# Attention in 64-row groups: scores as split products, transposes as two halves, spread reciprocals, v products in three pieces

## The chip, the cores and the metric

The kernel runs on one core of a Trainium2 chip. The metric is the time of one execution on the device in microseconds (us), the median of several runs. PE is the matrix engine (its weight loads have a row of their own, PEld), DVE the vector engine, ACT the scalar engine, POOL the GpSimd engine, SP the engine whose queue issues most DMAs.

## What is computed

Three stages follow one another. The first is attention with a learned bias, for 4 batches, 8 heads, 576 positions, head size 64; the second and third are dense layers over the 4 x 576 = 2304 tokens of width 512.

```python
scores = scale * np.matmul(q, k.transpose(0, 1, 3, 2))
...
scores = scores + bias.transpose(2, 0, 1)[None, :, :, :]
scores = scores - np.max(scores, axis=-1, keepdims=True)
attn = np.exp(scores)
attn = attn / (np.sum(attn, axis=-1, keepdims=True) + 1e-09)
return np.matmul(attn, v).astype(np.float32)
...
x = np.ascontiguousarray(attn_out.transpose(0, 2, 1, 3)).reshape(B * S, H * D)
x = _moe_ref(x=x, **moe_kwargs)
return _moe2_ref(x=x, **moe2_kwargs)
```

The middle layer multiplies by 512 x 1024 weights, applies h * softmax(h) and a layer norm, and multiplies by 1024 x 512 weights. The last one multiplies by 512 x 2048 weights, applies a clipped square, and multiplies by 2048 x 512 weights. All is float32; large products are made of a high part in the PE format fp32r and a low remainder.

## The kernel before

A head part (up to about 52 us) makes the bias and writes it to DRAM. Then come 16 **units**, one for each head pair `hp` and batch `b` (`u = 4 * hp + b`), then the middle layer (18 blocks of 128 tokens), then the last layer. The change touches attention, and the transposes and outputs of the middle layer.

**Inputs.** `load_qk` (L213) brings q and k of one head, each as [64, 640] and each stored twice, in partitions 0 to 63 and 64 to 127, with one DMA of 640 KB into one of two stage buffers. `prep_all` (L228) is a generator of four steps per head: DVE casts k to `kh`, the remainder goes to `kl` (DVE for the first unit, POOL later), DVE casts q to `sq`, and the lower 64 partitions of `sq` become the remainder of q. So `sq` holds the high part of q in 64 rows and the low part in the other 64, and two products over 128 rows, with `kh` and with `kl`, give the whole score.

**A unit** has nine row blocks `n` of 128 rows: four for each head, and block 8 with the last 64 rows of both. `k = 9 * u + n`.
- `emit_qk` (L379): the matmuls of a block (L392), 288 columns each, into the two banks of `ps_s` (two such buffers): 4, or 8 for block 8. Then one DVE instruction (L398) adds the bias, writes the negated scores `e` and takes their minimum into `su`.
- `emit_exp` (L410): ACT's exponential in place, with the row sums into `su`.
- `emit_T` (L486): four 128x128 transposes of a block into a bank of `ps_t` (three buffers, L497), copied to `pt` by ACT (L498); single blocks for the columns 512 to 575 (L504, L505, L511), copied by ACT and, for block 8, by DVE (L507, L508).
- `emit_pv` (L514): products with v (L529), 64 rows of output for each head, 256 columns at a time in two groups, and 64 columns for block 8. ACT copies the first 512 columns to `xb` (L536), DVE the last 64 (L538).
- `emit_norm` (L460): `r` makes the reciprocals of the row sums on DVE (L464, L465) and spreads them over 64 columns on POOL (L466); `R` transposes them on PE (L474), `M` multiplies `xb` by them on DVE (L476); `S` and `N` do the same for block 8 (L479, L484).

**The order** is written by hand: one string of letters for each of the nine blocks (`order`, L621), in which Q is `emit_qk`, E `emit_exp`, T the transposes of the block five before, P the v products of a group seven before, B a step of `prep_all`, W a step of the splitting of the middle layer's weights (`split_w`, L311), and r, R, M, S, N the normalization of the unit before. Every engine takes its instructions in this order. After the last block the same loop runs on with `tail`, mixed with the first two token blocks of the middle layer (`emit_h`, `emit_post`).

**The middle layer** uses the same PSUM pool: `emit_h` takes a `ps_s`, `emit_lt` (L821) transposes eight 128x128 blocks (L835) into two `ps_t`, and `emit_o` (L844) puts 48 products (L854) into `ps_x`, which has one buffer.

Of the kernel before, what the change touches and what calls it, by code (L numbers as in the profile page):

```python
# [28 lines left out]
QW = S + 64  # L29
NU = HP * B  # L30
# [8 lines left out]
def tile_attention_moe_moe(  # L39
# [168 lines left out]
    EB, LT, LP = 4, 5, 7  # L208


    kh_t, kl_t, sq_t, v_t, stg_t = {}, {}, {}, {}, {}

    def load_qk(s, eng=nc.sync):  # L213
        if s < 2 * NU:
            u, h = divmod(s, 2)
            hp, b = divmod(u, B)
            st = wq.tile([128, 2 * QW], F32, tag="stg", name="stg", bufs=2)
            eng.dma_start(out=st, in_=qk[b, 2 * hp + h])
            stg_t[s] = st
# [7 lines left out]

    def prep_all():  # L228
        for s in range(2 * NU):
            u, h = divmod(s, 2)  # L230
            st = stg_t.pop(s)
            n = S + 64 * h
            kh = wq.tile([128, n], F32R, tag=f"kh{h}", name="kh", bufs=2)
            kl = wq.tile([128, n], F32R, tag=f"kl{h}", name="kl", bufs=2)
            sq = wq.tile([128, QW], F32R, tag="sq", name="sq", bufs=4)
            ks = st[:, QW:QW + n]
            nc.vector.tensor_copy(kh, ks)
            yield
            eng = nc.vector if u == 0 else nc.gpsimd
            eng.tensor_tensor(out=kl, in0=ks, in1=kh.bitcast(F32), op=ALU.subtract)  # L240
            nc.vector.tensor_copy(sq, st[:, 0:QW])  # L241
            yield
            eng.tensor_tensor(
                out=sq[64:128], in0=st[64:128, 0:QW], in1=sq[64:128].bitcast(F32), op=ALU.subtract
            )
            kh_t[s], kl_t[s], sq_t[s] = kh, kl, sq
            load_qk(s + 2)
            yield
            yield

# [126 lines left out]
    e_t, su_t, r_t, pt_t, x_t = {}, {}, {}, {}, {}  # L377

    def emit_qk(k, sc=None):  # L379
        u, n = divmod(k, 9)  # L380
        hp, b = divmod(u, B)
        sc = sc or ps_s()
        i, h0 = divmod(n, 2)
        for hf in range(2):
            parts = []
            for h in ([h0] if n < 8 else [0, 1]):
                lhs = sq_t[2 * u + h][:, 128 * i:128 * i + 128]
                c0 = hf * HS + (64 if h == 1 and n == 8 else 0)
                for kk in (kh_t[2 * u + h], kl_t[2 * u + h]):
                    parts.append((lhs, kk[:, c0:c0 + HS]))  # L390
            for j, (l, r) in enumerate(parts):
                nc.tensor.matmul(sc[:, hf, 0:HS], lhsT=l, rhs=r, start=j == 0, stop=j == len(parts) - 1)  # L392
        if n % 2 == 0:
# [3 lines left out]
        e = e_t[u, i][:, h0, :]  # L397
        nc.vector.tensor_tensor_reduce(  # L398
            out=halves(e),
            in0=sc[:, :, 0:HS],  # L400
# [19 lines left out]
    for p in range(NB + 2):  # L420
# [9 lines left out]
        if p in first:  # L430
            emit_qk(first[p], ps0.tile([128, 2, 512], F32, tag="zz", name="zz", bufs=1))
        elif p - 1 in first:
            emit_exp(first[p - 1])
# [20 lines left out]
    def ps_t():  # L454
        return ps.tile([128, 512], F32, tag="t", name="ps_t", bufs=3)

    def ps_x():
        return ps.tile([128, 512], F32, tag="x", name="ps_x", bufs=1)

    def emit_norm(u, c):  # L460
        su, x = su_t[u], xb_t[u % B][:, u // B] if c in "MN" else None
        rc = su[:, 18:27]
        if c == "r":
            nc.vector.tensor_scalar(out=rc, in0=su[:, 9:18], scalar1=1e-9, scalar2=None, op0=ALU.add)  # L464
# [5 lines left out]
        elif c == "R":  # L470
            r_t[u] = r = ps_t()
            rb = flat(e_t.pop((u, 4)))[:, S:S + 512]
            for i in range(4):
                nc.tensor.transpose(r[:, 128 * i:128 * i + 128], rb[:, 128 * i:128 * i + 128], ident)  # L474
        elif c == "M":
            nc.vector.tensor_tensor(out=x[:, 0:512], in0=x[:, 0:512], in1=r_t.pop(u), op=ALU.mult)  # L476
        elif c == "S":
            r_t[u, 1] = r = ps_t()
            nc.tensor.transpose(r[:, 0:128], rc[:, 8:9].to_broadcast([128, 128]), ident)  # L479
        elif c == "N":  # L480
            r = r_t.pop((u, 1))
            for h in range(2):
                hs = slice(64 * h, 64 * h + 64)
                nc.vector.tensor_tensor(out=x[hs, 512:S], in0=x[hs, 512:S], in1=r[hs, hs], op=ALU.mult)  # L484

    def emit_T(k):  # L486
        u, n = divmod(k, 9)
        i, h = divmod(n, 2)
        e = flat(e_t[u, i])
        g, o = divmod(i, 2)  # L490
        if n in (0, 4, 8):
            pt_t[u, g] = wa.tile([128, 9, 256], F32, tag="pt", name="pt", bufs=2)
        pt = pt_t[u, g]
        tp = ps_t()
        for kt in range(4):
            c0 = (S + 64) * h + kt * 128
            nc.tensor.transpose(tp[:, kt * 128:(kt + 1) * 128], e[:, c0:c0 + 128], ident)  # L497
# [16 lines left out]
    def emit_pv(u, g):  # L514
# [4 lines left out]
        if g != 1:  # L519
            x_t[u] = ps_x() if g == 0 else ps_t()  # L520
# [104 lines left out]
    for k in range(NK + LP + 1):  # L625
# [32 lines left out]
        if k > NK:  # L658
            step(bp)
# [561 lines left out]
```

## Time and profile before

| | |
|---|---|
| median of 3 runs | 916.93 us (915.68 to 918.5) |
| the profiled execution, its own time | 915.25 us |
| its span, first to last instruction | 913.5 us |
| head, up to the first steady matmuls of attention | about 52 us |
| attention with its end | about 52 to 325 us |
| middle layer | about 325 to 532 us |
| last layer | about 532 to 913.5 us |
| PE, DVE, ACT, POOL busy | 902.6, 711.9, 604.1, 255.8 us |

The profile is of one execution. A duration of DVE or ACT runs from its start to the acknowledgement of its last write, so that one instruction overlaps the next a little. The ends of matmuls are modelled and they overlap much, so that the distance from one start to the next tells more than the duration. The chain that ended last is followed back from the last instruction; a piece of it counts the time from its start to the next piece's.

### The profile page before, as it was taken

To read this page: it belongs to the slowest core of one execution; us is meant where nothing else is said; L and a number is where in the kernel's file an instruction comes from. 1 tells how busy PE (TensorE), PEld (TensorE's weight loads), DVE (VectorE), ACT (ScalarE), POOL (GpSimd) and SP (SyncE) were. 2 spreads that over 40 slices of the span, in tenths; PEclk is the share of its full clock that TensorE was granted. 3 is DMA by queue.
4 is the path that set the end of the run, shared out by engine and by line. 5 is a ranking of instruction groups with operands and counts; after the bars stand their busy time and mean duration, and the time that the engine had idled before them with its cause. 6 is when DMAs were issued, how large, how long until landed. Compare 5 with 4: busy or idle time off the path is not lost.

```text
span 913.5 us, 17850 instructions
## 1 busy us (share of the span) xinstructions
PE 902.6 (99%) x6538; PEld 791.3 (87%) x6538; DVE 711.9 (78%) x1534; ACT 604.1 (66%) x1262; POOL 255.8 (28%) x231
## 2 busy tenths in 40 slices
PE   9989999999999999999999999999999999999998
PEld 6668888888888889999999998888898889888896
DVE  9968888989898548888988258888887875677864
ACT  7889898999999766677676544655455443455442
POOL 1036566565755223545366400000000000000000
PEclk9999999999999999999999999999999999999999
DMA  6994654744741102555653678769577765448541
GB/s 192 315 318 128 204 179 152 240 149 140 245 158 51 36 24 94 185 197 185 242 206 137 223 252 308 263 198 326 171 233 252 264 222 162 124 150 257 172 161 70
DMA packets 102523, 173.21 MB, mean 190 GB/s; under 512 B 11618, under 2 KB 66402, under 8 KB 102436
## 3 DMA queue, kind: packets, MB, share of 16 engines
q1 hardware_dynamic: 96000, 165.70, 55.2%
q10 hardware_dynamic: 6068, 4.73, 1.5%
q0 software_dynamic: 368, 1.64, 0.5%
q8 instruction: 52, 0.85, 0.4%
q14 instruction: 35, 0.29, 0.1%
HBM read 125.49 MB, written 46.54 MB: 188 GB/s over the span
## 4 chain that ended last, share of the span: by engine, by line
PE 80%; DVE 7%; ACT 6%; issue 3%; DMA 2%; POOL 1%; ACTq 0%; DVEq 0%; SPq 0%
PE acc L1026 20%; PE ab L988 18%; PE ps_s L392 10%; PE ps_x L529 8%; PE ps_t L497 7%; PE ps_s L575 6%; PE ps_x L854 4%; DMA bias_d<-ow 2%; ACT r L286 1%; POOL wp L723 1%; PE ps_s L854 1%; DVE wp L720 1%; PE ps_t L474 1%; PE ps_t L529 1%; DVE wp L712 1%
## 5 line engine op out<-in xcount | busy, mean ns | idle before, releaser
L1026 PE MATMUL acc<-wo,gh 128*128 128x512 f32 x576 | 179.3, 392 | 0.0
L398 DVE CUSTOM_DVE_ANT_0 e<-ps_s,bt 128x576 f32<-128x576 f32 x143 | 106.9, 748 | 20.2 <-PE ps_s L392 16.3
L1026 PEld LDWEIGHTS acc<-wo,gh 128*128 128x128 f32 x576 | 105.8, 188 | 14.5 <-DVE ob L1011 0.7
L413 ACT ACTIVATE e<-e,su 128x576 f32<-128x576 f32 x144 | 112.6, 782 | 7.4 <-DVE su L398 6.8
L1026 PE MATMUL acc<-wo,gl 128*128 128x512 f32 x288 | 114.5, 398 | 0.3 <-DVE gl L975 0.3
L392 PE MATMUL ps_s<-kh,sq 128*128 128x288 f32 x318 | 100.3, 333 | 3.3 <-ACT ow L303 2.0
L974 ACT CAST gh<-ga 128x384 fp32r<-128x384 f32 x96 | 49.4, 515 | 75.0 <-DVE ga L968 75.0
L498 ACT COPY pt<-ps_t 128x512 f32<-128x512 f32 x144 | 83.6, 582 | 10.5 <-PE ps_t L497 8.8
L392 PE MATMUL ps_s<-kl,sq 128*128 128x288 f32 x318 | 89.4, 298 | 0.0
L963 ACT ACTIVATE ga<-cs,half_c 128x384 f32<-128x384 f32 x72 | 44.4, 616 | 62.0 <-DVE cs L959 62.0
L988 PE MATMUL ab<-x2d,wr 128*128 128x384 f32 x288 | 84.7, 335 | 0.6 <-DVE cs L959 0.6
L497 PE MATMUL ps_t<-ident,e 128*128 128x128 f32 x576 | 84.0, 273 | 0.0
L975 DVE TENSOR_TENSOR gl<-ga,gh 128x384 fp32r<-128x384 f32 x96 | 53.1, 553 | 34.9 <-ACT gh L974 34.7
L954 ACT COPY pk<-ab 128x384 f32<-128x384 f32 x96 | 45.2, 471 | 47.3 <-PE ab L988 47.2
L529 PE MATMUL ps_x<-pt,v 128*64 128x256 f32 x640 | 76.2, 384 | 0.0
L854 PE MATMUL ps_x<-lh,woh 128*128 128x256 f32 x256 | 73.3, 286 | 0.1
L854 PE MATMUL ps_x<-lh,wol 128*128 128x256 f32 x256 | 72.1, 281 | 0.0
L854 PE MATMUL ps_x<-ll,woh 128*128 128x256 f32 x256 | 72.0, 281 | 0.0
L959 DVE TENSOR_TENSOR cs<-ab,pk 128x384 f32<-128x384 f32 x72 | 39.8, 553 | 39.1 <-PE ab L988 38.9
L497 PEld LDWEIGHTS ps_t<-ident,e 128*128 128x128 f32 x576 | 69.7, 141 | 0.6 <-ACT e L594 0.4
L392 PEld LDWEIGHTS ps_s<-kh,sq 128*128 128x128 f32 x318 | 60.6, 191 | 10.3 <-DVE sq L241 5.4
L1026 PEld LDWEIGHTS acc<-wo,gl 128*128 128x128 f32 x288 | 54.0, 187 | 12.4 <-DVE gl L975 1.0
(200 smaller groups left out, 2321.6 us busy)
## 6 DMA issues: line engine op xcount, KB each, us to landing
wr<-wi_d SPq DMA_DIRECT2D x168, 256.0 KB, 3.8
stg<-in_qk_dram SPq DMA_DIRECT2D x30, 640.0 KB, 3.9
raw<-in_w2nd_dram SPq DMA_DIRECT2D x32, 512.0 KB, 4.3
wi_d<-wd SPq DMA_DIRECT2D x24, 512.0 KB, 5.7
bias_d<-ow SPq DMA_DIRECT2D x36, 295.5 KB, 4.9
wo_d<-wd SPq DMA_DIRECT2D x16, 512.0 KB, 4.0
wo<-wo_d SPq DMA_DIRECT2D x16, 512.0 KB, 5.5
st<-x_d SPq DMA_DIRECT2D x16, 384.0 KB, 5.6
```

Source lines behind the costliest of these rows:

```text
L392: nc.tensor.matmul(sc[:, hf, 0:HS], lhsT=l, rhs=r, start=j == 0, stop=j == len(parts) - 1)
L398: nc.vector.tensor_tensor_reduce(out=halves(e), in0=sc[:, :, 0:HS], in1=halves(b_t[hp, n]), scale=-1.0 / float(D) ** 0.5, scalar=3.0e38, o ...
L413: nc.scalar.activation(out=e, in_=e, func=ACTF.Exp, scale=-1.0, bias=su[:, n:n + 1], accum_out=su[:, 9 + n:10 + n])
L497: nc.tensor.transpose(tp[:, kt * 128:(kt + 1) * 128], e[:, c0:c0 + 128], ident)
L498: nc.scalar.copy(out=pt[:, 4 * h:4 * h + 4, 128 * o:128 * o + 128], in_=tp.rearrange("p (a b) -> p a b", a=4))
L529: nc.tensor.matmul(x[64 * h:64 * h + 64, o0:o0 + w], lhsT=v[:, kt, 64 * h:64 * h + 64], rhs=r, start=kt == 0, stop=kt == 4, skip_group_che ...
L575: nc.tensor.matmul(h[:, hf, :], lhsT=l[:, kk, :], rhs=r[:, kk, c0:c0 + 512], start=kk == 0 and j == 0, stop=kk == KD - 1 and j == 2,)
L854: nc.tensor.matmul(ob[:, a * 256:(a + 1) * 256], lhsT=l, rhs=r[:, f, :], start=f == 0 and j == 0, stop=f == K1 - 1 and j == 2,)
L974: nc.scalar.copy(out=gh, in_=a)
L975: nc.vector.tensor_tensor(out=gl, in0=a, in1=gh.bitcast(F32), op=ALU.subtract)
L988: nc.tensor.matmul(d, lhsT=l, rhs=r[:, kk], start=q in (1, 2, 5) and kk == 0 and m == 0, stop=kk == 1 and m == 2, skip_group_check=True,)
L1026: nc.tensor.matmul(d, lhsT=l, rhs=r, start=first and m == 0, stop=last and m == 2, skip_group_check=True)
```

## The change

1. **Stage and split.** The stage tile has 640 columns of q and 352 of k (`KW = HS + 64`): in partitions 0 to 63 the first 352 columns of k, in 64 to 127 those from column 288 on. Three DMAs bring them. High part `hi` and remainder `lo` are made for q and k alike, all 128 rows.
2. **Scores.** Three products (high by high, high by low, low by high) in place of two over stacked rows. Each is made as two matmuls of 64 rows, one for each half of the columns, on partitions 0 to 63 into one bank and on 64 to 127 into the other. The product of the two low parts is no longer made.
3. **Transposes.** `turn` transposes a block as two matmuls of 64 rows, one into each of two banks. A `ps_t` now has two banks, and there are two of them. Five large transposes per unit (T0 to T4) of eight blocks, each copied by one ACT copy of 1024 columns. T4 holds block 8 and the spread reciprocals. Single blocks go to free columns of a score buffer (`carry`), and DVE copies them.
4. **Normalization.** Block 8 is multiplied by its reciprocals before it is transposed. x is multiplied by the transposed reciprocals as it leaves PSUM; the ACT copy of x is gone.
5. **v products** with 512 columns, in the pieces P0, P1, P2, and `p` for block 8, all into one `ps_t`.
6. **Order.** One list for a whole unit, in which scores (Q), their reduction (D) and exponentials (E) are separate entries; another list for the end.
7. **Middle layer.** `emit_lt` transposes into one two-bank `ps_t`, `emit_o` takes a `ps_t` instead of `ps_x`.

```diff
+            eng.dma_start(out=st[0:64], in_=src[0:64, 0:QW + KW])
+            eng.dma_start(out=st[64:128, 0:QW], in_=src[64:128, 0:QW])
+            eng.dma_start(out=st[64:128, QW:QW + KW], in_=src[64:128, QW + HS:2 * QW])
...
+            eng = nc.vector if s < 2 else nc.gpsimd
+            for part in (slice(QW, QW + KW), slice(0, QW)):
+                nc.vector.tensor_copy(hi[:, part], st[:, part])
+                yield
+                eng.tensor_tensor(out=lo[:, part], in0=st[:, part], in1=hi[:, part].bitcast(F32), op=ALU.subtract)
...
-            for j, (l, r) in enumerate(parts):
-                nc.tensor.matmul(sc[:, hf, 0:HS], lhsT=l, rhs=r, start=j == 0, stop=j == len(parts) - 1)
...
+            for l, r in ((hi, hi), (hi, lo), (lo, hi)):
+                parts.append((l[:, 128 * i:128 * i + 128], r[:, c0:c0 + HS]))
+        for j, (l, r) in enumerate(parts):
+            for hf in range(2):
+                rows = slice(64 * hf, 64 * hf + 64)
+                nc.tensor.matmul(sc[:, hf, 0:HS], lhsT=l[rows], rhs=r[rows], start=j == 0, stop=j == len(parts) - 1)
...
+        return ps.tile([128, 2, 512], F32, tag="t", name="ps_t", bufs=2)
+
+    def turn(dst, c, src):
+        for r in range(2):
+            rows = slice(64 * r, 64 * r + 64)
+            nc.tensor.transpose(dst[:, r, c:c + 64], src[rows], ident[rows, rows])
...
+    def carry(key, src):
+        held[key] = sc = sc_t[-1] if sc_t else ps_s()
+        turn(sc, HS, src)
...
+            for j in range(8):
+                h, kt = divmod(j, 4)
+                turn(tp, 64 * j, e[:, (S + 64 * (i < 4)) * h + 128 * kt:][:, 0:128])
...
+            nc.scalar.copy(out=dst.rearrange("p k (a c) -> p k a c", a=2), in_=tp)
...
+            rc = su_t[u][:, 18:27]
+            nc.vector.tensor_scalar(out=rc, in0=su_t[u][:, 9:18], scalar1=1e-9, scalar2=None, op0=ALU.add)
             nc.vector.reciprocal(out=rc, in_=rc)
             nc.gpsimd.tensor_copy(
                 e_t[u, 4][:, 1, 0:512].rearrange("p (i d) -> p i d", i=8),
                 rc[:, 0:8].unsqueeze(2).to_broadcast([128, 8, 64]),
             )
...
+            e = e_t[u, 4][:, 0, :]
+            nc.vector.tensor_scalar(out=e, in0=e, scalar1=rc[:, 8:9], scalar2=None, op0=ALU.mult)
+        elif m == "P":
...
+            for kt in ((0, 1), (2, 3), (4,))[i]:
+                for h in range(2):
+                    nc.tensor.matmul(
+                        x_t[u][64 * h:64 * h + 64, 0], lhsT=v[:, kt, 64 * h:64 * h + 64],
+                        rhs=pt[:, 8 if kt == 4 else 4 * h + kt],
+                        start=kt == 0, stop=kt == 4, skip_group_check=True,
+                    )
...
+                nc.vector.tensor_tensor(
+                    out=x[:, 0:512], in0=x_t[u][:, 0], in1=flat(e_t[u, 4])[:, 512:1024], op=ALU.mult
                 )
...
+    order = """
+        Q B D r Q T2 Q C2 D m3 T3 D E C3 k3 Q T4 D W B B B Q E b W E B C4 Q D P0 d P1 p E W P2 W W D
+        E Q M m0 W T0 N Q D E k0 C0 E m1 Q B m2 D k1 B E D T1 k2 W E C1 B W
+    """.split()
+    late = "T2 T3 T4 C2 C3 C4 m3 k3 b d r N M P0 P1 P2 p".split()
...
+    for c in "H T2 C2 m2 k2 H r T3 C3 m3 k3 O W b d T4 C4 O P0 P1 P2 p O M N O H O H".split():
...
-        ob = ps_x() if p < NTT // 2 - 2 or half == 0 else ps_s()[:, 0, :]
+        ob = (ps_t() if p < NTT // 2 - 2 or half == 0 else ps_s())[:, 0, :]
```

In the new list the entries of `late` belong to the unit before, the others to the unit itself. C is the ACT copy of a large transpose, m and b are transposes of single blocks, k and d their DVE copies.

## Rows read from the trace of the kernel before

**Rows 1.** The page's totals and the chain that ended last, whole span.

```profile
PE 902.6 (99%) x6538; PEld 791.3 (87%) x6538; DVE 711.9 (78%) x1534; ACT 604.1 (66%) x1262; POOL 255.8 (28%) x231
...
PE 80%; DVE 7%; ACT 6%; issue 3%; DMA 2%; POOL 1%; ACTq 0%; DVEq 0%; SPq 0%
```

**Rows 2.** The chain of waits in order of time: start, us, what; v products.

```profile
68.22 2.31 PE ps_x L529 x20
...
291.56 2.31 PE ps_x L529 x20
```

**Rows 3.** Two stretches: us, busy PE, PEld, DVE, ACT, POOL; clock, DMA share, GB/s.

```profile
131.90:147.85 15.95, 15.95 (x149) 13.86 (x148) 14.02 (x39) 14.34 (x37) 9.90 (x9) 1.00 0.42 137
243.60:259.55 15.95, 15.95 (x148) 13.84 (x146) 14.31 (x39) 15.22 (x39) 10.07 (x9) 1.00 0.66 203
```

**Rows 4.** The chain of waits from 300 to 350 us.

```profile
300.10 0.58 PE ps_t L529 x20
...
301.26 0.44 PE ps_t L497 x4
301.70 0.56 PE ps_s L392 x4
...
303.89 1.06 PE ps_s L392 x8
...
312.11 2.31 PE ps_x L529 x20
...
344.60 5.70 PE ps_x L854 x48
```

**Rows 5.** Waits of all engines, 68.2 to 305 us: total us, times, longest.

```profile
DVE e L398 <- PE ps_s L392: 12.4, 30, 1.4
...
PEld ps_s L392 <- DVE sq L241: 5.4, 14, 0.4
...
PEld ps_x L529 <- issue: 5.0, 30, 0.2
```

**Rows 6.** Weight loads of two lines of the head: ns minimum/median/maximum, first and last start.

```profile
L170 PEld LDWEIGHTS zz<-x,onea x4: 325/326/328, 3.1 to 3.8; 2*128 2x128 f32 x4
...
L153 PEld LDWEIGHTS o<-wt x18: 287/333/338, 1.1 to 6.5; 128*128 128x128 f32 x18
```

**Rows 7.** Timeline of ACT in one unit: start us, us, instruction.

```profile
143.05 0.59 ACT L498 COPY pt<-ps_t 128x512 f32<-128x512 f32 x1 [0.33 <-PE ps_t L497]
143.53 0.27 ACT L512 COPY pt<-ps_t 128x128 f32<-128x128 f32 x1
143.69 0.79 ACT L413 ACTIVATE e<-e,su 128x576 f32<-128x576 f32 x1
```

**Rows 8.** Timeline of DVE in the same unit.

```profile
132.90 0.45 DVE L237 CAST kh<-stg 128x576 fp32r<-128x576 f32 x1
133.27 0.48 DVE L241 CAST sq<-stg 128x640 fp32r<-128x640 f32 x1
...
134.34 0.71 DVE L464 TENSOR_SCALAR su<-su 128x9 f32<-128x9 f32 x1
...
141.10 0.21 DVE L538 COPY xb<-ps_t 128x64 f32<-128x64 f32 x1
141.70 0.69 DVE L476 TENSOR_TENSOR xb<-xb,ps_t 128x512 f32<-128x512 f32 x1 [0.39 <-PE ps_t L474]
...
145.07 0.45 DVE L484 TENSOR_TENSOR xb<-xb,ps_t 64x64 f32<-64x64 f32 x2
145.55 0.76 DVE L398 CUSTOM_DVE_ANT_0 e<-ps_s,bt 128x576 f32<-128x576 f32 x1
146.23 0.08 DVE L398 DVE_READ_ACCUMULATOR2_ANT su<- 128x1 f32 x1
```

**Rows 9.** SP's waits, 68.2 to 305 us, and the page's row of stage loads.

```profile
SPq L218 <- POOL sq L243: 73.0, 23, 4.8
...
stg<-in_qk_dram SPq DMA_DIRECT2D x30, 640.0 KB, 3.9
```

More of the change, by code (lines that the diff above doesn't have):

```diff
@@ L226, in load_v @@
             v_t[u] = v
[L228 to L249, printed above, removed]
     b_t = {}
@@ L430, in tile_attention_moe_moe @@
         if p in first:
-            emit_qk(first[p], ps0.tile([128, 2, 512], F32, tag="zz", name="zz", bufs=1))
+            emit_q(first[p], ps0.tile([128, 2, 512], F32, tag="zz", name="zz", bufs=1))
+            emit_d(first[p])
         elif p - 1 in first:
@@ L454, in ps_t @@
     def ps_t():
[L455 to L464, printed above, removed]
+        return ps.tile([128, 2, 512], F32, tag="t", name="ps_t", bufs=2)
@@ L469, in emit_norm @@
             )
[L470 to L484, printed above, removed]
@@ new lines, in tile_attention_moe_moe @@
+    order = """
[3 more added lines that the diff above has]
+    late = "T2 T3 T4 C2 C3 C4 m3 k3 b d r N M P0 P1 P2 p".split()
+    w_n = 0
+    for u in range(NU):
+        n = {"Q": 9 * u, "D": 9 * u, "E": 9 * u}
+        for j, c in enumerate(order):
+            if c in n:
+                k = n[c]
+                n[c] += 1
+                if k not in first.values():
+                    {"Q": emit_q, "D": emit_d, "E": emit_exp}[c](k)
+                if c == "D" and u % B == B - 1 and u // B + 1 < HP:
+                    load_bias(u // B + 1, k % 9)
+                if u == NU - 1 and c == "E" and k % 9 in (1, 5):
+                    split_x(k % 9 // 5)
@@ L652, in tile_attention_moe_moe @@
             elif c == "B":
                 step(bg)
-            elif c == "W" and k >= 6:
-                step(bw)
-        if k in (NK - 8, NK - 6):
-            split_x(0 if k == NK - 8 else 1)
-        if k > NK:
-            step(bp)
-        if k == NK + LT - 1:
-            drain(emit_h(1))
-            drain(bp)
-            es_q.close()
-            es_b, wb = opened(pool("wb"))
-            split_x(2)
-            bp = emit_post(1)
-        elif k == NK + LT + 1:
-            split_x(3)
@@ L669, in tile_attention_moe_moe @@
-        if n == 5 and 1 <= u < NU - 1:
-            load_v(u + 1)
+            elif c == "W":
+                if w_n >= 4:
+                    step(bw)
+                w_n += 1
+            elif c not in late:
+                emit_late(u, c)
+            elif u > 0:
+                emit_late(u - 1, c)
+    hs = chain(emit_h(0), emit_h(1))
+    bp = None
+    for c in "H T2 C2 m2 k2 H r T3 C3 m3 k3 O W b d T4 C4 O P0 P1 P2 p O M N O H O H".split():
+        if c in late:
+            emit_late(NU - 1, c)
+        elif c == "W":
+            drain(bw)
+        elif c == "H":
+            step(hs)
+        elif c == "O":
+            bp = bp or emit_post(0)
+            step(bp)
@@ L673, in tile_attention_moe_moe @@
+    drain(bp)
+    es_q.close()
+    es_b, wb = opened(pool("wb"))
+    split_x(2)
+    bp = emit_post(1)
+    split_x(3)
     w2p_t, kept = {}, set()
```

196 lines of the change are left out of this document (88 added, 108 removed).

## The prediction

> **What bounds the kernel now.** I read the page's totals first. PE is busy almost all of the span and carries 80% of the chain that ended last [rows 1], so I looked for the stage that the change touches and asked whether PE ever waits there. Attention works through 16 units (one head pair of one batch each). The first of each unit's two runs of v products starts at 68.22 us and, 14 units later, at 291.56 [rows 2]: (291.56 - 68.22) / 14 = 15.95 us for one unit. Two such stretches side by side [rows 3] show PE busy for the whole 15.95, DVE for 14.02 and 14.31, ACT for 14.34 and 15.22 (the second half also scales the weights), POOL for 10. So PE sets the pace with two engines close behind it, and each engine works its list in order.
>
> A busy PE says little, since its durations overlap. The chain gives what one instruction really costs, because it counts from start to start [rows 4]: four score matmuls 0.56 and eight 1.06, so 0.134 each; four transposes 0.44, so 0.109 each; twenty v products of 256 columns 2.31, twenty of 64 columns 0.58. A unit has 40, 46, 40 and 20 of these: 5.4 + 5.0 + 4.6 + 0.6 = 15.6 us. The rest of the 15.95 is short waits, of which the table of waits [rows 5] names two: 5.4 us for the cast of q and 5.0 us of issue before v products, over 15 units 0.7 together (part of it is inside the 2.31).
>
> The v products also show that tiles of the array work side by side. A float32 matmul is two instructions in this trace (40 for 20 calls). One transpose of 128 columns costs 0.109, so 256 columns alone would cost 0.218 and twenty 4.4. They cost 2.31: the two heads, in two column halves, run together. No instruction of before runs as two row halves.
>
> **The change, part by part.** Durations come from the profiled execution, 915.25 us; the median of the three runs is 916.93. I apply the difference to the median.
>
> *Scores.* Four 128-row matmuls per row block become three products in two halves of 64 rows, in two banks: six matmuls for a block, 60 instead of 40 per unit, in 30 pairs. If a pair runs side by side it costs what one costs now, 0.134: 30 x 0.134 = 4.0 us, 1.4 less. Bounds for a pair: 0.134 (the streaming of 288 columns does not shrink) and 0.268 (no overlap). I take 0.134, nearest to the row of the v products, where pairs do overlap.
>
> *Transposes.* Each becomes two halves of 64 rows: 45 pairs per unit (40 in the five large blocks, which now hold the spread reciprocals, 4 single ones and the last block's), against 46. The streamed identity shrinks from 128 to 64 columns, the stationary operand keeps its 128. How long a load takes is the question. In the head a load with 2 rows has a median of 0.326 us, one with 128 rows 0.333 [rows 6]: rows don't matter, columns do. So I take 0.109 for a pair whose two loads overlap: 45 x 0.109 = 4.9. Bounds: 0.055 (streaming alone) and 0.218 (loads one after the other). The Trainium skill, "TensorE: Matmul & The Clock Gate", section on LDWEIGHTS, says the same of loads (time by columns, whatever the rows), and the row agrees; its Part 3 says that loads overlap matmuls in flight when the row groups differ, which no run here shows yet. By the first alone a split transpose doubles; by both together it costs what it cost.
>
> *v products.* 512 columns instead of two times 256, in three pieces one behind another: the same columns, 2 x 2.31 less one entry of some 0.1, so 4.5, and 0.6 for the narrow ones. PE per unit: 4.0 + 4.9 + 4.5 + 0.6 = 14.0, with 0.2 of short waits 14.2 us. If nothing else bound, 1.75 us a unit would go.
>
> *ACT.* From one start to the next a 128x512 copy takes 143.53 - 143.05 = 0.48, a 128x128 one 0.16 [rows 7]. So a column costs (0.48 - 0.16) / 384 = 0.00083, and a copy of 1024 about 0.16 + 896 x 0.00083 = 0.91. Nine of 0.48 (4.3) become five of 0.91 (4.5); four small ones (0.64) go to DVE; the copy of x (0.48) goes, since x is scaled straight out of PSUM. Together -0.9: 13.4 in the first half, 14.3 in the second. ACT is no bound.
>
> *DVE* [rows 8]. Away: the two 64x64 multiplications at the end (0.45); the casts of k shrink from 576 and 640 columns (0.37 by starts: 132.90 to 133.27) to 352 (0.25), -0.25 for two. Added: four copies of single blocks out of PSUM, 0.22 each by the 128x64 copy (0.21), bounds 0.16 and 0.28, 0.9 together; the multiplication of the last block by its reciprocals, 128x576, which no row shows: at best like the cast of 576 columns (0.37), at worst like the 128x9 operation that took 0.71 (a small operation, so most of that is waiting), I take 0.5. The two small copies stay, and the product into x stays (0.69). Sum +0.7: 14.0 to 14.3 becomes 14.7 to 15.0. DVE now has more to do than PE.
>
> *The order.* The v products now stand in one block on PE: 4.5 + 0.6 = 5.1 us in which no new scores come. What can DVE do meanwhile? Between the fourth reduction and the product into x its list has two reductions (0.68 each: 145.55 to 146.23), the two small copies (0.45) and nine of a unit's sixteen weight and q/k steps. These sixteen are what is left of 14.7 after nine reductions (6.1), the single blocks (0.9), the small copies (0.45), the products and copies into x (0.9) and the reciprocals with their multiplication (0.71 + 0.1 + 0.5): 5.0 us, so nine are 2.8. Together 4.6 of the 5.1: DVE idles 0.5 us per unit, because the product into x waits for the block's end. The other 10.1 us of DVE work stand beside 9.1 of PE. So a unit takes 5.1 + 10.1 = 15.2 us, with DVE as the bound; two score buffers could hide a part of the 0.5. Before, ACT ran at 15.22 of 15.95 and no PE matmul waited for it in the steady units, so lists this full are possible.
>
> *Queues and the rest.* The staging load becomes three DMAs, 64 more over the run, smaller by 22%. SP mostly waits there for POOL to free the stage buffer (73.0 us over 23 waits), and a load lands after 3.9 us [rows 9], so two issues more are hidden in that wait; if the cover were gone, a late load would hold the next cast. The six loads of the head on GpSimd's queue come long before their use. POOL gets 352 + 640 columns instead of 576 or 640 + 640: slightly less. In the stage after attention the eight transposes of a token block share one two-bank tile and the output takes the other: PE's work there is the same (48 products in 5.70 [rows 4]) and a buffer is asked for again only a block later, so nothing. The end of attention orders the same work anew; I count 0, with 2 us either way.
>
> *Sum.* (15.95 - 15.15) x 15 periods = 12 us: 915.25 - 12 = 903.3 against the profiled run, 916.93 - 12 = 904.9 for the median. Forecast 905.
>
> **The rivals.**
>
> *Row halves do not overlap in loading (slower).* Place: each pair of 64-row loads, 75 per unit. Price: a pair costs two loads, 0.218. Scores 30 x 0.218 = 6.5, transposes 45 x 0.218 = 9.8, with the rest 6.5 + 9.8 + 4.5 + 0.6 + 0.2 = 21.6 us: (21.6 - 15.95) x 16 = 90 us, 1007 us. For: loads depend on columns, and no row halves are in the trace. Against: loads for column halves do overlap (twenty narrow products in 0.58, 0.029 each). It decides early: PE is back at 15.95 when a pair costs (15.95 - 14.2) / 75 = 0.023 more than I take. The section of the Trainium skill on LDWEIGHTS named above, taken alone, gives this case. Chance 0.16.
>
> *The reciprocals come late.* The last block's transposes wait for reduction, exponential, reciprocal on DVE, the spread on POOL. The first DVE step there already takes 0.71 for nine columns [rows 8]; the added multiplication stands right behind it. If it waits as long, and PE waits for the spread, one unit gains 0.8 to 1.2 on 15.2: 16.0 to 16.4, 918 to 924 us. For: DVE has no slack left. Against: on PE ten other pieces stand between. Chance 0.16, mostly within the bound.
>
> *The loads are cheaper than the transposes show.* If streaming was what took 0.109, a pair of halves costs some 0.06, PE falls to 12, and DVE alone at 14.7 sets the pace: (15.95 - 14.7) x 15 = 19 us, 898. Against: the two-row loads. Chance 0.1.
>
> *Main case*: 0.58, by itself 895 (a unit of 14.5) to 912 (15.6).
>
> **How the numbers follow.** A measurement tells 0.3%, 2.75 us, from no change. Faster: main case and cheaper loads, 0.68. Same: two thirds of the late reciprocals, 0.11. Slower: row halves that don't overlap and the rest, 0.21. The range goes from 895 (main case at its best) to 923 (late reciprocals) and leaves out the 0.16 of the first rival and some hundredths below.
>
> **What would show it.** Right: starts of the v products 15.2 us apart; six score matmuls in about 0.40 us and sixteen half transposes in about 0.87; PE waiting for DVE before scores, which it does not do now (in the waits DVE waits for PE instead, 12.4 us [rows 5]); DVE near 14.7 of 15.2. Wrong: half transposes at twice that (first rival), PE waits before the last block's transposes (second), 0.5 for sixteen halves (third). If the period is right and the time is not, the head or the end of attention has moved by more than 2 us.

## The result and the profile after

| | before | after |
|---|---|---|
| median, side by side on one chip | 916.3 us (915.31 to 918.5) | 902.83 us (899.54 to 906.16) |
| ratio, 95% interval | | 0.985 (0.981 to 0.989) |
| profiled execution, its time / span | 915.25 / 913.5 | 899.54 / 897.6 |

Faster by 13.5 us, 2.2 us below the forecast of 905. The forecast's total is near; its terms are not, as the rows show.

Against [rows 1]: PE's busy time falls by 40 us, DVE's by only 4, and PE's share of the chain that ended last falls from 80% to 49%. The row of stage loads is the first of the three DMAs.

```profile
PE 862.6 (96%) x7242; PEld 720.1 (80%) x7242; DVE 708.0 (79%) x1582; ACT 586.5 (65%) x1118; POOL 240.6 (27%) x235
...
PE 49%; DVE 8%; ACT 5%; issue 2%; POOL 1%; ACTq 0%; DVEq 0%
...
stg<-in_qk_dram SPq DMA_DIRECT2D x30, 248.0 KB, 3.5
```

Where the 15.9 us of span went, cut at three marks of PE's timeline (starts, us): the first and fifteenth block of narrow v products, and the first matmul of the last layer.

| stretch | before | after | difference |
|---|---|---|---|
| start to the first narrow products | 76.52 | 78.14 | +1.6 |
| 14 unit periods | 223.41 (15.96 each) | 204.22 (14.59 each) | -19.2 |
| the end of attention and the middle layer | 231.84 | 233.57 | +1.7 |
| last layer | 381.7 | 381.7 | 0 |

So the units give 19.2 us, where the forecast had 15.15 us a unit and thus 11.2 for these fourteen, and 3.3 us are given back around them. Of the fourteen periods eleven take 14.30 to 14.39 us and three 15.43 to 15.45. Three of them in the windows view (columns as in [rows 3]), first a long one, then two of the steady ones:

```profile
122.19:137.62 15.43, 13.54 (x192) 9.43 (x190) 15.01 (x46) 13.23 (x27) 9.49 (x10) 1.00 0.45 123
137.62:151.94 14.32, 13.36 (x193) 9.37 (x191) 13.69 (x42) 13.34 (x27) 8.82 (x10) 1.00 0.50 133
253.60:267.97 14.37, 13.41 (x192) 9.34 (x190) 13.71 (x42) 14.11 (x30) 8.76 (x10) 1.00 0.48 132
```

DVE has 13.69 of 14.32 us, PE 13.36 by durations that overlap. PE's timeline of one unit gives its real price, from start to start:

```profile
132.00 0.40 PE L386 MATMUL ps_s<-hi 64*128 64x288 f32 x2 [0.34 <-DVE su L397]
132.24 0.29 PE L386 MATMUL ps_s<-lo,hi 64*128 64x288 f32 x2
132.37 0.29 PE L386 MATMUL ps_s<-hi,lo 64*128 64x288 f32 x2
132.50 0.66 PE L460 MATMUL ps_t<-ident,e 64*128 64x64 f32 x16
132.97 0.39 PE L386 MATMUL ps_s<-hi 64*128 64x288 f32 x2
...
134.14 3.65 PE L518 MATMUL ps_t<-pt,v 128*64 128x512 f32 x16
137.62 0.75 PE L528 MATMUL ps_t<-e,v 128*64 128x64 f32 x20
138.21 1.03 PE L518 MATMUL ps_t<-pt,v 128*64 128x512 f32 x4
139.17 0.40 PE L386 MATMUL ps_s<-hi 64*128 64x288 f32 x2
```

A pair of score halves starts 0.13 after the last (132.24 to 132.37), as forecast, but the first pair of a block takes 0.24, so that the three pairs of a block take 132.50 - 132.00 = 0.50 where the forecast had 0.40. Sixteen half transposes take 132.97 - 132.50 = 0.47, that is 0.059 a pair, little more than half of the 0.109 that I took; the v block takes 139.17 - 134.14 = 5.03. PE now waits for DVE ahead of scores (the first row). The waits of the steady part, 75 to 290 us, say the same; in [rows 5] DVE waited for PE instead:

```profile
PE ps_s L386 <- DVE pt L491: 11.1, 29, 1.1
PEld ps_s L386 <- DVE su L397: 8.4, 20, 0.6
...
PE ps_s L386 <- DVE su L397: 5.6, 17, 0.4
...
DVE hi L231 <- DMA stg<-in_qk_dram: 1.5, 2, 1.1
```

**DVE's list is shorter than forecast, though the added work costs what I took** (the last block's multiplication 0.52 us). Same instructions, same shapes, other durations: groups of DVE instructions by form, 80 to 270 us, first before (mean in ns behind the total), then after:

```profile
L241 DVE CAST sq<-stg 128x640 fp32r<-128x640 f32 x24 | 19.9, 829 | 0.0
...
L464 DVE TENSOR_SCALAR su<-su 128x9 f32<-128x9 f32 x12 | 8.6, 715 | 0.0
```

```profile
L231 DVE CAST hi<-stg 128x640 fp32r<-128x640 f32 x26 | 12.6, 485 | 0.0
...
L504 DVE TENSOR_SCALAR su<-su 128x9 f32<-128x9 f32 x13 | 2.2, 167 | 0.0
```

Two casts and one small operation per unit: 2 x (0.829 - 0.485) + 0.715 - 0.167 = 1.24 us of DVE less, with no change to them at all. In the trace of before the long ones stand beside an instruction of POOL: the 0.71 us for nine columns [rows 8] began at 134.34, while POOL subtracted from 133.48 to 135.03. After, they stand where POOL waits. The long units, next, and the last three experiments bear on this cause.

**The long units** follow a late stage. Of the 26 casts of 352 columns between 80 and 270 us, 23 take 0.33 to 0.34 us; the three late ones, at 89.85, 120.61 and 163.83, take 1.68, 0.68 and 1.52. DVE's timeline at two of them, then POOL's:

```profile
118.98 0.49 DVE L231 CAST hi<-stg 128x640 fp32r<-128x640 f32 x1
120.61 0.68 DVE L231 CAST hi<-stg 128x352 fp32r<-128x352 f32 x1 [1.15 <-DMA stg<-in_qk_dram]
...
163.83 1.52 DVE L231 CAST hi<-stg 128x352 fp32r<-128x352 f32 x1 [0.31 <-DMA stg<-in_qk_dram]
```

```profile
119.54 1.55 POOL L233 TENSOR_TENSOR lo<-stg,hi 128x640 fp32r<-128x640 f32 x1 [1.65 <-DVE hi L231]
...
163.60 1.55 POOL L233 TENSOR_TENSOR lo<-stg,hi 128x640 fp32r<-128x640 f32 x1 [1.64 <-DVE hi L231]
```

SP's timeline of the load for the first of them:

```profile
113.50 0.55 SPq L220 DMA_DIRECT2D stg<-in_qk_dram  x1
114.11 0.59 SPq L221 DMA_DIRECT2D stg<-in_qk_dram  x1
115.29 0.47 SPq L222 DMA_DIRECT2D stg<-in_qk_dram  x1
```

The third of the three DMAs is issued 1.8 us after the first. DVE's wait for it is 1.15 us in one case and 0.31 in the other, and yet both units are longer by 1.1: a cast that is late starts behind POOL's subtraction of 640 columns and ends 0.2 us after it, however late it was (120.61 + 0.68 against 119.54 + 1.55; 163.83 + 1.52 against 163.60 + 1.55). The third case, some 0.2 us late, ends 0.2 us after POOL too. At the start of the 23 short ones no subtraction of POOL is under way.

### The profile page after: what moved, and what is told of

It reads as the page before. It is cut to its first block, busy times and chain, and to the rows that moved or that the text cites. A ratio compares the mean times of both kernels' runs of the same rounds, so it can differ in the third digit from the quotient of the medians.

```text
span 897.6 us, 19361 instructions
## 1 busy us (share of the span) xinstructions
PE 862.6 (96%) x7242; PEld 720.1 (80%) x7242; DVE 708.0 (79%) x1582; ACT 586.5 (65%) x1118; POOL 240.6 (27%) x235
## 4 chain that ended last, share of the span: by engine, by line
PE 49%; DVE 8%; ACT 5%; issue 2%; POOL 1%; ACTq 0%; DVEq 0%
PE acc L1026 21%; PE ab L988 18%; PE ps_t L854 4%; PE ps_s L580 3%; POOL wp L724 1%; PE ps_s L854 1%; DVE wp L721 1%; ACT eb L599 1%; DVE raw L712 1%; ACT wp L717 1%; ACT scb L616 1%; ACT lh L839 1%; DVE wd L696 1%; PE ps_t L834 1%; DVE wp L713 1%
## 5 line engine op out<-in xcount | busy, mean ns | idle before, releaser
L233 POOL TENSOR_TENSOR lo<-stg,hi 128x352 fp32r<-128x352 f32 (+1 forms) x60 | 75.4, 1257 | 97.3 <-DVE hi L231 97.3
L386 PE MATMUL ps_s<-hi 64*128 64x288 f32 x318 | 62.9, 383 | 24.2 <-DVE pt L491 11.2
L518 PE MATMUL ps_t<-pt,v 128*64 128x512 f32 x320 | 74.8, 597 | 0.0
L854 PE MATMUL ps_t<-lh,woh 128*128 128x256 f32 x256 | 73.3, 286 | 0.6 <-DVE stb L610 0.6
L854 PE MATMUL ps_t<-lh,wol 128*128 128x256 f32 x256 | 72.1, 282 | 0.0
L854 PE MATMUL ps_t<-ll,woh 128*128 128x256 f32 x256 | 72.1, 282 | 0.0
L386 PEld LDWEIGHTS ps_s<-hi 64*128 64x128 f32 x318 | 32.7, 190 | 48.1 <-issue 16.0
L487 ACT COPY pt<-ps_t 128x1024 f32<-128x1024 f32 x64 | 64.1, 1002 | 5.4 <-PE ps_t L460 5.4
L967 DVE SCALAR_TENSOR_TENSOR ga<-ga 128x384 f32<-128x384 f32 x96 | 53.2, 555 | 11.9 <-ACT ga L963 11.9
L988 PE MATMUL ab<-x2b,wr 128*128 128x384 f32 x240 | 57.0, 335 | 0.0
```

Of the source, the lines that this page charges most:

```text
L233: eng.tensor_tensor(out=lo[:, part], in0=st[:, part], in1=hi[:, part].bitcast(F32), op=ALU.subtract)
L386: nc.tensor.matmul(sc[:, hf, 0:HS], lhsT=l[rows], rhs=r[rows], start=j == 0, stop=j == len(parts) - 1)
L487: nc.scalar.copy(out=dst.rearrange("p k (a c) -> p a k c", a=2), in_=tp)
L518: nc.tensor.matmul(x_t[u][64 * h:64 * h + 64, 0], lhsT=v[:, kt, 64 * h:64 * h + 64], rhs=pt[:, 8 if kt == 4 else 4 * h + kt], start=kt == ...
L854: nc.tensor.matmul(ob[:, a * 256:(a + 1) * 256], lhsT=l, rhs=r[:, f, :], start=f == 0 and j == 0, stop=f == K1 - 1 and j == 2,)
L967: nc.vector.scalar_tensor_tensor(out=a, in0=a, scalar=1.0, in1=a, op0=ALU.min, op1=ALU.mult)
```

## The experiments

Two questions stood first: which part of the change gives the gain, and what took back a part of it. Each kernel below was timed beside the kernel before on the same chip; ratios are to that one, unit periods are starts of the narrow v products. "After" is the changed kernel.

### Whole transposes

```diff
-                turn(tp, 64 * j, e[:, (S + 64 * (i < 4)) * h + 128 * kt:][:, 0:128])
+                nc.tensor.transpose(flat(tp)[:, 128 * j:128 * j + 128], e[:, c0:c0 + 128], ident)
```

> The 40 large transposes of a unit are made whole again (128 rows, 128 streamed columns); all else as after the change. In the trace after the change sixteen halves take 0.47 us, 0.059 for a pair, where a whole transpose took 0.109 before: 40 x 0.05 = 2.0 us more of PE per unit. Theory A (PE and the points at which it and DVE wait for each other set the unit; PE idles about 1.0 us of 14.37): half to all of the 2.0 shows, a unit of 15.3 to 16.3, 918 to 933 us, so the change would gain nothing without this part. Theory B (DVE alone paces, as the prediction had it): PE's 2.0 us fit beside DVE's work, a unit of 14.4 to 15.0, 903 to 912 us. Theory C (a pair of halves costs what a whole one costs): no change, 903 us.

Only the 40 large transposes of a unit are changed; the single blocks stay halves. Measured: 917.8 us, ratio 1.0017 (1.0007 to 1.0026), unit periods 15.67 but for three of 16.17 to 16.25. PE's timeline, and the windows of one unit:

```profile
180.41 0.29 PE L386 MATMUL ps_s<-hi,lo 64*128 64x288 f32 x2
180.63 1.09 PE L481 MATMUL ps_t<-ident,e 128*128 128x128 f32 x8
181.66 0.40 PE L386 MATMUL ps_s<-hi 64*128 64x288 f32 x2
```

```profile
158.19:173.86 15.67, 15.67 (x152) 10.84 (x150) 13.87 (x42) 13.21 (x28) 8.79 (x10) 1.00 0.67 197
```

Eight whole transposes occupy PE for 1.03 us, with the scores around them in halves, and the first starts 0.22 after the last score product instead of 0.13. Without the half transposes nothing of the gain is left: PE is the bound again, busy for the whole 15.67 us, and DVE waits for scores (6.2 us in 13 waits, 75 to 290 us).

### Products of one half first, then of the other

```diff
-        for j, (l, r) in enumerate(parts):
-            for hf in range(2):
+        for hf in range(2):
+            for j, (l, r) in enumerate(parts):
```

> The same score products, but all of one row half first, then all of the other, so that neighbours share their rows of the array. Theory A (the gain of the scores comes from two row halves running side by side, 0.134 us a pair): 60 x 0.134 = 8.0 instead of 4.0 us of PE per unit, less about 1.0 of idle time: a unit 3 to 4 us longer, 950 to 967 us. Theory B (order does not matter, PE overlaps halves by itself from its queue, or each half is half as long): 903 us.

Measured: 904.19 us, ratio 0.9878 (0.9853 to 0.9903), units of 14.66 to 14.73 but for two late ones; no more than a fraction of the gain hangs on the order in which the halves are issued. The score block with twelve products (six of one half, then six of the other, then a single block's transposes, then sixteen half transposes):

```profile
186.62 0.37 PE L386 MATMUL ps_s<-hi 64*128 64x288 f32 x1 [1.08 <-DVE pt L491]
...
186.96 0.41 PE L386 MATMUL ps_s<-hi 64*128 64x288 f32 x2
...
187.54 0.22 PE L460 MATMUL ps_t<-ident,e 64*128 64x64 f32 x1
187.59 0.29 PE L386 MATMUL ps_s<-lo,hi 64*128 64x288 f32 x1
187.60 0.26 PE L460 MATMUL ps_t<-ident,e 64*128 64x64 f32 x1
187.72 0.29 PE L386 MATMUL ps_s<-hi,lo 64*128 64x288 f32 x1
```

The second half's first product starts about when the first half's fourth does ("x2" at 186.96), and transposes of one half, at 187.54 and 187.60, start before score products of the other that were issued earlier, at 187.59 and 187.72. The two row halves work off their instructions apart from each other.

### Stacked scores, half transposes

Scores and their inputs as before the change, all else as after.

```diff
-        for j, (l, r) in enumerate(parts):
-            for hf in range(2):
-                rows = slice(64 * hf, 64 * hf + 64)
-                nc.tensor.matmul(sc[:, hf, 0:HS], lhsT=l[rows], rhs=r[rows], start=j == 0, stop=j == len(parts) - 1)
+        for hf in range(2):
...
+                    parts.append((sq[:, 128 * i:128 * i + 128], kk[:, c0:c0 + HS]))
+            for j, (l, r) in enumerate(parts):
+                nc.tensor.matmul(sc[:, hf, 0:HS], lhsT=l, rhs=r, start=j == 0, stop=j == len(parts) - 1)
```

> The scores as before the change (high and low part stacked in 128 rows, two products, one stage DMA of 640 KB, casts of 576 or 640 columns of k), everything else as after it. PE 40 x 0.134 = 5.4 instead of 4.0 us per unit, DVE 0.2 more. Theory A (PE's order with DVE): 0.4 to 1.4 us per unit, 909 to 925 us. Theory B (DVE alone): 0.2 per unit, 905 to 907 us.

Measured: 922.15 us, ratio 1.0058 (1.0035 to 1.0081), units of 15.93.

```profile
181.89 0.29 PE L392 MATMUL ps_s<-kl,sq 128*128 128x288 f32 x1
182.11 0.71 PE L466 MATMUL ps_t<-ident,e 64*128 64x64 f32 x16
182.75 0.40 PE L392 MATMUL ps_s<-kh,sq 128*128 128x288 f32 x1
```

Sixteen half transposes now hold PE for 182.75 - 182.11 = 0.64 instead of 0.47, and begin 0.22 after a product that takes 0.13: 0.26 us for going from 128-row matmuls to halves and back. The Trainium skill, "TensorEngine Tiling (Array Packing)", section "Key Properties", says that changing the tiling mode drains the engine; the 0.09 us before the halves and the 0.17 after them agree. So neither part alone gives anything: the scores in halves without the transposes leave 917.8, the transposes without the scores 922.15, both together 902.83.

### One DMA for a stage

The input is laid out on the host as the stage tile wants it.

```diff
-            eng.dma_start(out=st[0:64], in_=src[0:64, 0:QW + KW])
-            eng.dma_start(out=st[64:128, 0:QW], in_=src[64:128, 0:QW])
-            eng.dma_start(out=st[64:128, QW:QW + KW], in_=src[64:128, QW + HS:2 * QW])
+            eng.dma_start(out=st, in_=src)
```

> The inputs are laid out so that one DMA of 496 KB brings the stage tile, instead of three. After the change three units of 15.4 instead of 14.3 us have a cast on DVE that waits up to 1.2 us for the stage load, whose third DMA was issued about 1.5 us after the first, between bias loads. Theory A (the issue of three DMAs on SP's queue makes it late): those waits go, 3 us less, about 900 us. Theory B (the DMA engines are full of bias loads then, at 0.85 share): the same late landing, 903 us.

Measured: 894.57 us (892.48 to 895.87), ratio 0.976 (0.974 to 0.978), 8 us below after, more than the 3 of Theory A, and faster than both kernels. No wait of DVE for the stage is left in the steady part; periods are 14.30 to 14.38 but for two (14.74 and 16.39, the latter with a stretch of half clock), and the first narrow products start at 75.51 instead of 78.14. The bytes are the same. Of the three DMAs each lands 3.5 or 3.6 us after its own issue (medians, 75 to 290 us) and they take 0.47, 0.59 and 0.59 us to issue; in the repeat below the one DMA takes 0.33 to issue and lands after 3.4. So what the three lose is mostly their place in the queue. The one DMA also brings longer rows, which no run tells apart from its single issue.

The changed kernel was then run again, and later this one again:

> The changed kernel once more, unaltered, beside the next three on one chip. Its runs so far lie between 899.5 and 906.2 us, more apart than those of before, and the mean granted clock goes with them (0.996 for the fastest, 0.992 for the slowest). Theory A (stretches at half clock after idle PE make the spread): again some 6 us between fastest and slowest, in step with the clock. Theory B (the one stage DMA run was faster because of its chip): about 896 here.

Measured: 902.16 us (898.86 to 906.96), ratio 0.986 (0.982 to 0.990); five units of 15.46 to 15.55 this time, and five waits of DVE for the stage, 3.4 us. So the chip was not the reason (Theory B). The spread came again, 8 us, and the slowest run has the lowest mean clock (0.986); but the fastest has 0.992, as the two between have, so the clock alone does not explain the spread.

> The kernel with one DMA for each stage once more, as the yardstick for the three beside it. Both theories expect 892 to 897 us and units of 14.30 to 14.38 us nearly throughout.

Measured: 894.21 us (892.19 to 894.9), ratio 0.9764 (0.9746 to 0.9783); first narrow products at 74.78, periods 14.30 to 14.38 but for two of 14.72 and 14.82. Against the profile of after its span is 6.0 us shorter: 3.4 us up to the first narrow products, 2.6 in the fourteen periods. By the medians the three DMAs cost 8 us, and both places show a part.

### A warm first unit

The first units of after run at half clock in two stretches of 3.4 us, before in one. Ahead of the first PE was busy for 4.13 of 7.20 us, ahead of the second for 1.33 of 3.40. Repeated matmuls keep the array busy there.

```diff
-        for j, (l, r) in enumerate(parts):
+        for j, (l, r) in list(enumerate(parts)) * (8 if k == 1 else 1):
...
-            for j in range(8):
+            for j in list(range(8)) * (5 if u + i == 0 else 1):
```

> One stage DMA, and in the first unit PE repeats the products of its second block eight times and one large transpose five times (about 4 us of repeated work) in the two stretches where it waits. Theory A (the half clock in the first unit comes from PE idling there, 6.8 us of it in the one-DMA run): the clock stays whole, 2 to 4 us less. Theory B (the clock falls whatever PE does there, or the time is set by the waits for loads): no gain, or up to 2 us more from the repeated work.

Measured: 895.23 us, ratio 0.9779 (0.9761 to 0.9797), beside 894.2 to 894.6 without the repeats: no gain. The windows at the place of after's half clock, PEclk behind the five engines:

```profile
57.20:60.60 3.40, 2.54 (x36) 1.84 (x34) 3.27 (x9) 2.93 (x8) 1.76 (x2) 1.00 0.95 308
...
64.00:67.40 3.40, 3.10 (x60) 2.76 (x58) 3.24 (x12) 3.40 (x8) 2.36 (x2) 1.00 0.50 170
```

The clock is whole, 2.4 GHz (after had 0.50 and 0.51 there, 1.2 GHz), and the time is the same. Whether the half clock alone cost anything this run can't tell, since the 4 us of repeated work stand in its place; and its profile has one late stage, with a unit of 15.51. The repeat of one DMA alone has a half-clock stretch of 6.8 us there and still reaches its first narrow products at 74.78, after (6.8 us in all) only at 78.14: what after lost up to that point was not the clock.

### What sets the unit now

Five more kernels, all with one DMA for a stage, move work between or within the engines' lists. The first puts the seventh block's scores into the v products, so that DVE has a reduction more to do there:

```diff
-        Q B D r Q T2 Q C2 D m3 T3 D E C3 k3 Q T4 D W B B B Q E b W E B C4 Q D P0 d P1 p E W P2 W W D
-        E Q M m0 W T0 N Q D E k0 C0 E m1 Q B m2 D k1 B E D T1 k2 W E C1 B W
+        Q B D r Q T2 Q C2 D m3 T3 D E C3 k3 Q T4 D W B B B Q E b W E B C4 Q D P0 d P1 Q p E W P2 W W D
+        E M m0 W T0 N Q D E k0 C0 E m1 Q B m2 D k1 B E D T1 k2 W E C1 B W
```

> One stage DMA, and the scores of the seventh block are made inside the v products, before the narrow ones, instead of behind them, so that DVE has a reduction ready while PE works through the block. Theory A (DVE idles some 0.3 us before the product into x, and PE waits about 1 us per unit for DVE afterwards, so the point where both meet sets the unit): 0.3 to 0.7 us less per unit, 5 to 10 us below the one-DMA kernel. Theory B (PE's and DVE's sums set it, each is already full): within 2 us of the one-DMA kernel.

Measured: 904.11 us, ratio 0.9877 (0.9856 to 0.9897), units of 15.04 to 15.13 but for one of 15.48, +0.74. Missed by both theories. DVE's timeline at the product into x, here and with one DMA alone:

```profile
197.42 0.69 DVE L537 TENSOR_TENSOR xb<-ps_t,e 128x512 f32<-128x512 f32 x1 [1.03 <-PE ps_t L516]
```

```profile
206.18 0.69 DVE L537 TENSOR_TENSOR xb<-ps_t,e 128x512 f32<-128x512 f32 x1 [0.29 <-PE ps_t L516]
```

Scores within the v products push their end back, the product into x waits for that end, and all that follows on DVE waits behind it: 1.03 - 0.29 = 0.74 us more idle, the unit's whole loss. The second gives the copies of single blocks to ACT in the first eight units:

```diff
-            nc.vector.tensor_copy(
+            (nc.scalar.copy if u < 8 else nc.vector.tensor_copy)(
```

> One stage DMA, and in the first eight units ACT instead of DVE makes the four copies of single blocks: DVE 0.9 us less per unit, ACT 0.6 more (it has 1.0 idle there). Theory A (DVE and the waits of PE for these copies, 11.2 us over the stage, set the unit): 0.4 to 0.9 us less in each of the first eight units, 3 to 7 us below the one-DMA kernel. Theory B (PE's own work sets it): no difference. Theory C (ACT's list is in the way, since the copies stand behind exponentials that wait): some us slower.

Measured: 905.19 us, ratio 0.989 (0.987 to 0.991); units of 15.80 where ACT copies (one of 16.15), 14.37 where DVE does. This is Theory C: on ACT the copies stand behind exponentials that wait for DVE, and PE waits for the copies:

```profile
PEld ps_s L384 <- ACT pt L489: 19.7, 28, 1.3
ACT pt L489 <- DVE su L395: 16.0, 7, 2.6
PE ps_s L384 <- ACT pt L489: 14.8, 28, 1.1
```

The other three take work off the stretch of DVE that follows the v products. One moves a cast into the v products, one gives the fifth block's multiplication to GpSimd, one does both:

```diff
-        Q B D r Q T2 Q C2 D m3 T3 D E C3 k3 Q T4 D W B B B Q E b W E B C4 Q D P0 d P1 p E W P2 W W D
-        E Q M m0 W T0 N Q D E k0 C0 E m1 Q B m2 D k1 B E D T1 k2 W E C1 B W
+        Q B D r Q T2 Q C2 D m3 T3 D E C3 k3 Q T4 D W B B B Q E b W E B C4 Q D P0 d P1 p E W P2 B W W D
+        E Q M m0 W T0 N Q D E k0 C0 E m1 Q m2 D k1 B E D T1 k2 W E C1 B W
```

> One DMA for each stage, and VectorE's cast of the stage (640 columns, 0.48 us) moved from between two score multiplications into the v products, where VectorE stands idle for some 0.3 us of each unit before the product into x. Theory A (VectorE sets the unit: its chain after the v products, and those 5.05 us themselves): the unit falls by the idle time, 0.2 to 0.3 us, and the span by 3 to 5 us, to 890 to 892 us. Theory B (TensorE at 13.4 of 14.3 us, or ScalarE at 13.3 to 14.1, holds it as closely): no change, 894 to 896 us.

```diff
+            nc.gpsimd.tensor_scalar(out=e, in0=e, scalar1=rc[:, 8:9], scalar2=None, op0=ALU.mult)
             nc.gpsimd.tensor_copy(
...
-            nc.vector.tensor_scalar(out=e, in0=e, scalar1=rc[:, 8:9], scalar2=None, op0=ALU.mult)
```

> One DMA for each stage, and the multiplication of the fifth block's e by its reciprocals (0.52 us of VectorE in each unit) given to GpSimd, ahead of the spreading of the reciprocals; GpSimd is busy 8.8 of 14.3 us. Theory A (VectorE sets the unit): units 0.5 us shorter in the first half, where ScalarE has 13.4 us, and 0.2 to 0.3 us shorter in the second, where it has 14.1; together 4 to 6 us less, 888 to 891 us. Theory B (TensorE and ScalarE hold the unit as closely, or GpSimd's later spreading delays the transposes): 894 to 898 us.

> One DMA for each stage, with both moves: the cast into the v products and the fifth block's multiplication on GpSimd. Theory A (VectorE sets the unit): units of 13.6 to 13.8 us in the first half and of 14.1 in the second, where ScalarE's own sum is 14.1; 885 to 889 us. Theory B: 894 to 898 us, and then neither engine's own sum but the chain across them sets the unit.

Measured, with ratios to the kernel before (the repeat of one DMA alone, on the same chip, had 894.21 us): the cast 909.07 us, ratio 0.9931 (0.9916 to 0.9946); the multiplication 899.06, 0.9816 (0.9801 to 0.9831); both 923.38, 1.0108 (1.0061 to 1.0155). All are slower than either theory said, the second by 1 us only. The kernel with the cast moved, DVE's timeline and then POOL's in the v products:

```profile
198.85 0.83 DVE L321 TENSOR_SCALAR wp<-raw 128x256 uint32<-128x256 uint32 x1
199.71 1.05 DVE L324 SCALAR_TENSOR_TENSOR raw<-raw,wp 128x256 f32<-128x256 uint32 x1
200.79 0.71 DVE L325 TENSOR_SCALAR wp<-raw 128x256 uint32<-128x256 uint32 x1
```

```profile
198.66 0.87 POOL L334 TENSOR_TENSOR wp<-raw,wp 128x256 f32<-128x256 f32 x1 [0.42 <-POOL lo L231]
199.49 0.98 POOL L231 TENSOR_TENSOR lo<-stg,hi 128x352 fp32r<-128x352 f32 x1
200.58 0.77 POOL L311 TENSOR_TENSOR wol<-wp,woh 128x256 fp32r<-128x256 f32 x1
```

These three steps of the weight splitting take 0.29, 0.43 and 0.29 us where POOL is idle. Here each begins while POOL computes and ends 0.15 to 0.29 us after the POOL instruction beside it. They were not touched by the edit; it moved a cast, with it POOL's subtraction, and so set POOL's work beside them. Mean durations of the three forms, 80 to 270 us, for two sets per unit:

| kernel | L321, L324, L325 ns | per unit, us | DVE against one DMA, per unit | unit, us |
|---|---|---|---|---|
| one DMA (first run) | 285, 659, 295 | 2.48 | | 14.33 |
| cast moved | 550, 737, 502 | 3.58 | +1.10 | 15.48 (+1.15) |
| multiplication on GpSimd | 388, 866, 606 | 3.72 | +1.24 - 0.52 = +0.72 | 14.76 (+0.43) |
| both | 681, 973, 730 | 4.77 | +2.29 - 0.52 = +1.77 | 16.43 (+2.1) |

In the second row from below the idle time ahead of the product into x (0.29) swallowed a part: 0.72 - 0.29 = 0.43. The windows of single units say the same without a sum of durations: DVE is busy for 13.66 of 14.30 us with one DMA, for 14.74 of 15.49 with the cast moved, 14.39 of 14.76 with the multiplication moved, 15.45 of 16.16 with both. So the unit follows DVE's list, as one theory had it, and what that list costs depends on what POOL does at the time. With both moves the clock was also halved in stretches; four units of 16.15 to 16.17 at whole clock are 1.83 longer, near the table's 1.77. The longer ones, 16.43 to 16.80, hold a stretch of half clock or follow a unit that does; how the other 0.3 us of 2.1 come about is not shown.

The Trainium skill, "SBUF — State Buffer", section "Who interferes with whom", says that DVE in some of its modes and GpSimd share a pair of ports under an exclusive lock, and that whichever starts first holds it for its whole instruction. The rows agree: L321 took 0.83 instead of 0.29 and ended after POOL's instruction, as the late casts of after did. Which mode DVE was in no row tells.

## Why the prediction came out right, and where its steps failed

**The frame held.** PE paced before, DVE after; the change shortens the unit to DVE's list plus idle time; the end moves by little. The main case (895 to 912 alone) holds the result. But of its own signs only some came: PE waits for DVE before scores, and the v block is as long as forecast. The starts of the v products are 14.3 us apart in most units and 14.59 in the mean, not 15.2; sixteen half transposes take 0.47, which was the sign of the third rival; and DVE's list, forecast to grow by 0.7, became shorter.

**Transposes: mis-sized.** I took 0.109 for a pair of half transposes; it took 0.059, near the lower bound of 0.055. The step that failed is the reading of [rows 6]: the durations of a 2-row and a 128-row load, 0.326 and 0.333, told me that columns set the price of a load. They are the time from a load's start to its end; how soon the next may follow is another question, and the half transposes answer it: two loads of 128 columns and two products go by in 0.059. This is the third rival's mechanism, to which I gave 0.1. The first rival (0.218 a pair) is refuted by the same row. For the scores 0.134 from pair to pair was right, but the first pair of a block takes 0.24, which the sum left out: a block of six took 0.50 for 0.40. The v block was 5.03 against 5.1.

**Only beside the forecast's DVE did PE's sum decide little.** Its 14.2 us of PE were hidden under 15.15 of DVE. With DVE at 13.7 they would not have been: the kernel with whole transposes (eight in 1.03 us) has units of 15.67, with PE busy all the time. The 14.3 us needed both errors, PE's and DVE's.

**DVE: mis-sized, and this made the unit 14.3 and not 15.15.** The added work was sized well: the multiplication 0.52 for 0.5, the nine-column operation apart. What failed is "what is left of 14.7": I carried 0.71 us for nine columns and 0.8 for half of the casts over as the price of these instructions, though I wrote beside the first that most of it was waiting. It was: 0.167 now, and 0.485 for each cast, 1.24 us a unit less. 14.17 (the mean of [rows 3]) + 0.7 - 1.24 = 13.63; measured 13.69 and 13.71. The idle time ahead of the product into x was taken as 0.5 and is 0.29; with other gaps it is 14.32 - 13.69 = 0.63. That such times come from POOL's work beside them was shown in the other direction, by the late casts of after (0.34 us with no subtraction of POOL under way, up to 1.68 behind one) and by the three last kernels; no kernel gave before's instructions their short times without the rest of the change.

**The reciprocals** were not late: no wait of PE for them is among the largest. In the kernel with the multiplication on GpSimd PE's loads did wait for it, 14 times, 0.9 us at the longest.

**Queues: wrong.** I costed two more DMAs per stage at nothing, hidden in SP's wait, and named what would go wrong if the cover were gone: a late load that holds the next cast. That happened in three units of the profile and five of the repeat, and the first unit started later. Waits of some 0.2 to 1.5 us cost 1.1 to 1.2 each, since a cast that comes a little late is held behind POOL's subtraction: that price was not in the sum. One DMA instead of three gives 8 us back. My cover was SP's wait for POOL to free the buffer, 73 us in all [rows 9]; but a load can start only when that wait ends, so every issue after it is late by its place in the queue. The wait covered nothing.

**Middle layer and end of attention:** +1.7 us, within the 2 that I allowed.

So two errors of the same sign in the units (19.2 instead of 11.2 us) and one of the other sign in the queues met near the forecast. That the total came within 2.2 us is luck: with one DMA, as the forecast had priced the queues, the time is 894.2 to 894.6 us, just below its range.

## What to carry to other kernels

Split both the products and the transposes around them into row halves, or neither: a change of form in between gives the gain back. The price of a DVE instruction in a profile is the price at that place: before it goes into a sum, look at what POOL does at the same time, and count moved POOL work as work for DVE. A queue's wait for a buffer is no cover for more DMAs behind it: what comes after the wait is on the path of the next use.

## What the runs showed of the hardware

- Two row halves of the array work off their matmuls apart: with all six products of one half issued first, the other half still started 0.34 us after the first one did, and its scores were passed by transposes issued after them.
- A pair of transposes of 64 rows and 128 columns takes 0.059 us, a whole one 0.109 [rows 4]; a change from 128-row matmuls to halves and back costs about 0.26 us.
- One DVE step on 128x256 integers (L325) took 0.29 us with POOL idle and up to 0.92 beside its work, on average 0.73 in the kernel with both moves. A cast of 352 columns took 0.34 us, and up to 1.68 when it started behind a subtraction of POOL; it then ended 0.2 us after POOL's end in all three cases.
- Two stretches of half clock in the first unit, 6.8 us, filled with repeated matmuls until the clock was whole, gave no time back.
